# Both halves of layer 1 as Strassen products from the seventh chunk on, sums grown on copies in PSUM, and layer 2 in two PSUM banks

## The chip, the cores and the metric

The kernel runs on one core of one Trainium2 chip. The metric is device time in microseconds (us) for one execution. Before the change three runs gave 208.86, 209.4 and 210.07 us; the median is 209.4 us.

## What is computed

Inputs are q, k, v of shape (4, 8, 768, 64) (batch, heads, positions, head size), a norm gain of 512, and two weight matrices of 512 x 2048 and 2048 x 512; the output is float32 of shape (4, 768, 512).

```
scores = (q @ k.T) / sqrt(64), kept where the key is one of the first 4
         positions, or lies 0 to 127 positions behind the query
x   = softmax(scores) @ v, heads side by side           (4, 768, 512)
xn  = (x - mean(x)) / sqrt(var(x) + 1e-6) * g_ln
out = x + relu(xn @ w_ch1) @ w_ch2
```

Nearly all of the arithmetic is in the last line: layer 1 (512 to 2048, with relu) and layer 2 (2048 to 512).

## The kernel before

The 3072 rows are cut into 24 tiles of 128 rows and 12 chunks of two tiles, three chunks to a batch. In the code chunks count from 0: "the seventh chunk" is c = 6. The kernel has no loop on the chip. It creates some 1100 operations (`P.op`, line 84), each with the engine or engines that can do it, the buffers that it reads, writes or holds, and a function that emits its instructions. `Plan.run` (line 115) gives each an engine, a start and a place in the rings of buffers, by priorities and assumed costs; the program is emitted in the order of those starts (lines 1210 to 1238), and each engine executes its own part strictly in that order. The framework adds the semaphores for what an instruction reads and overwrites.

The engines are TensorE (PE, matmuls), VectorE (DVE), ScalarE (ACT), GpSimd (POOL) and SyncE (SP, which issues DMAs). PSUM has eight banks of 512 float32 columns: four in the two tiles of the ring `pair` (attention), four in the ring `one` (all else).

Per chunk, from c = 4 on:

- **Attention** (`attend`, line 777): scores by PE in two groups `sc..0`, `sc..1` (line 802), exp on ACT (814), mask on DVE or POOL (826, 821), sink values `sv` (721), values `av` (854), then on DVE the division (`rc`, `x`: 868, 870), mean and variance (`bn`, `ag`: 874, 876), and the normed rows `xc` (885); a transposing DMA makes `xnt`, 512 x 256 in bf16.
- **Layer 1** (`mlp`, line 1006, and `halves`, line 927). The 2048 columns lie in two halves g = 0, 1, of 1024 columns each, that end in the tiles `hq[0]` and `hq[1]`. The first half is a Strassen-type scheme of seven products m1 to m7 (line 958) instead of eight: 2 x 2 blocks of weights (512 columns by 256 inputs) against 2 x 2 blocks of tokens (128 by 256 inputs), with sums of weight blocks (`wsum`, line 923, once) and of token blocks (`xt`, on POOL, line 938, once per chunk). A product is eight matmuls of 128 columns. It uses three banks z, w, y: m1, m6, m7, m4 grow in z, m5 and m3 in y, m2 is alone in w. Between them ACT copies a bank to `tz` (969) for later use, DVE adds a bank and a `tz` into `hq` (980), and ACT clips that block at zero in place (983); the last block is clipped straight out of the bank (1001). The second half is plain: four units `ph` of eight 256-column matmuls (1027), each followed by one relu out of the bank, `rl` (1037 on ACT, 1039 on DVE).
- **Layer 2** (`wino`, line 1074, from c = 2 on): seven products p1 to p7 of eight 256-column matmuls (line 1109), with sums of blocks of `hq` (s1 to s4 for both halves, DVE, line 1092) and of the second weights (made once). It has four regions of 256 columns: z in the bank x, l2 and r1 in the bank y, l1 in the bank w. p1, p6, p5 grow in z, p7 and p4 in l2; p2 is l1 and p3 is r1. A `keep` (DVE, line 1123) adds a region and the rows x into a buffer `tm` in SBUF, a `final` (DVE, line 1130) adds a region and a `tm` into the output tile `ot`. Four of each make the chunk's two output tiles, which SP stores.

The order of PE's work before, from one chunk's end to the next, is regular: p1 p2 p7 p6 sc p4 p5 p3 of a chunk, then m1 sv av m5 m2 ph av m6 m3 ph m7 ph ph m4 of the next chunk, then that chunk's p1. After the last chunk's p3 there is one small matmul `late` (line 1206) that reads the last output, and the program ends with a branch on a flag.

Of the kernel before, what the change touches and what calls it, by code (L numbers as in the profile page):

```python
# [13 lines left out]
class Buf:  # L14


    def __init__(self, name, ring=None):
        self.name, self.ring = name, ring
        self.writers, self.users = [], []
        self.slot = None  # L20
        self.left = 0
# [6 lines left out]
class Unit:  # L28


    def __init__(self):
        self.free_at = 0.0
        self.lives = []
        self.held = False


class Slot:
# [12 lines left out]
    def take(self):  # L50
        for u in self.units:
            u.held = True
# [12 lines left out]
class Plan:  # L65


    SEM = 0.035
    TO_PE = 0.11
    PE_DRAIN = 0.18  # L70
    SWITCH = 0.095
    LANES = 8
    SHARED = 36.0
    MIXED = 1e9
    DMA_BUSY = {}
# [32 lines left out]
    def lat(self, src, dst):  # L108
        if src.eng == "PE" and src.dma is None:
            return -self.PE_DRAIN if dst == "PE" else self.SEM  # L110
        return self.TO_PE if dst == "PE" else self.SEM

    WINDOW = {"PE": 0.2, "ACT": 0.25, "DVE": 0.25, "POOL": 0.25, "SP": 0.0}

    def run(self):
        free = {"PE": 0.9, "ACT": 0.75, "DVE": 0.9, "POOL": 1.5, "SP": 0.75}
        lanes = {"POOL": [0.0] * self.LANES, "HW": [0.0] * self.LANES}
        n_dma = {"POOL": 0, "HW": 0}
        dma_free = {"POOL": 0.0, "HW": 0.0, "all": 0.0}
        mode = "n"  # L120
        ready = [o for o in self.ops if o.n_wait == 0]
        order = []
        tensor = sorted((o for o in self.ops if "PE" in o.engs), key=lambda o: (o.prio, o.seq))
        while ready:
            while tensor and tensor[0].start is not None:
                tensor.pop(0)
            head = tensor[0] if tensor else None
            cand = {}
            first = min([o.prio for o in ready for b in o.bufs if b.ring == "pair" and b.slot is None], default=1e9)
            for o in ready:  # L130
                if "PE" in o.engs and o is not head and o.prio >= PAR["strict"]:
                    continue
                need = [b for b in o.bufs if b.ring and b.slot is None]
                ok, avail, took = True, 0.0, {}
                for b in need:
                    used = [u for s in took.values() for u in s.units]
                    ss = [s for s in self.rings[b.ring] if not s.held and not any(u in used for u in s.units)
                          and not (s.lent and o.prio > first)]
                    if not ss:
                        ok = False  # L140
                        break
                    since = max([min(s.free_at for s in ss)] + [min(free[e] for e in o.engs) - 0.3])
                    s = min((s for s in ss if s.free_at <= since), key=lambda s: (s.rank, s.free_at))
                    took[b] = s
                    avail = max(avail, s.free_at)
                if not ok:
                    continue
                best = None
                for e, (occ, lat) in o.engs.items():
                    r = max([free[e], o.nb, avail + (self.TO_PE if e == "PE" else self.SEM)]  # L150
                            + [d.end + self.lat(d, e) for d in o.deps])
                    if e == "PE" and o.mode_in != mode:
                        r = max(r, free[e] + self.SWITCH)
                    if o.dma is not None:
                        q = "POOL" if e == "POOL" else "HW"
                        r = max(r, lanes[q][n_dma[q] % self.LANES])
                    if best is None or r + lat < best[0] - 1e-9:
                        best = (r + lat, e, r)
                cand.setdefault(best[1], []).append((best[2], o, took))
            if not cand:  # L160
                stuck = sorted(ready, key=lambda o: o.prio)[:8]
                raise RuntimeError("plan stuck: " + ", ".join(
                    f"{o.name}[{','.join(b.name for b in o.bufs if b.ring and b.slot is None)}]" for o in stuck))
            e = min(cand, key=lambda e: min(c[0] for c in cand[e]))
            t0 = min(c[0] for c in cand[e])
            st, o, took = min((c for c in cand[e] if c[0] <= t0 + self.WINDOW[e]), key=lambda c: (c[1].prio, c[1].seq))
            for b, s in took.items():
                b.slot = s
                s.take()
            o.eng, o.start = e, st  # L170
            occ, lat = o.engs[e]
            free[e] = st + occ
            if e == "PE":
                mode = o.mode_out
            if o.dma is None:
                o.end = st + lat
# [1103 lines left out]
```

## Time and profile before

| | us |
|---|---|
| median of three runs | 209.4 |
| lowest, highest | 208.86, 210.07 |
| span of the profiled execution, first to last instruction | 206.6 |
| the median above that span | 2.8 |

The profiled execution has no time of its own on the page beside its span; the 2.8 us are what the median of the runs shown has more. The granted TensorE clock of the core was 1.000 as a mean.

How to read the rows. The page begins with the busy time of each engine (PE for matmuls, PEld for weight loads, which run beside matmuls). In the rows by group, the order is line, engine, operation, `out<-in` by the program's names without numbers, shape and count; then busy us and mean ns of one; then the engine's idle time just before, and what ended it. In a timeline the first column is the start in us from the start of the span, the second the time to the group's end, and square brackets hold the idle time before and who ended it; matmuls overlap, so their price is the distance from one start to the next. In a windows row the window is followed by its length, then PE, PEld, DVE, ACT and POOL busy (with counts), the granted clock, the DMA share and GB/s. A row of waits says who waited for whom, us in total, how often, and the longest.

### The profile page before, as it was taken

The page shows a single profiled execution, that of the slowest core. Times are in us where ns is not written, and L with a number is a line of the kernel's source. Part 1 is how long each engine was busy: PE and PEld are TensorE (multiplying, and loading weights), DVE is VectorE, ACT ScalarE, POOL GpSimd, SP SyncE. Part 2 cuts the span into 40 slices and gives each one's busy share as a digit, 9 for nine tenths or more (in the row PEclk, how much of TensorE's full clock was granted, in tenths as well). Part 3 has the DMA queues.
Part 4 walks back from the last instruction along what each step waited for, and adds up shares of the span by engine and source line. Part 5 has one row for each costly group of instructions (what it writes and reads, how often), then busy time and mean ns, then how long its engine had stood idle before and what let it go on. Part 6 is the DMA issues. An engine that isn't in the chain of part 4 may idle for free.

```text
span 206.6 us, 6790 instructions
## 1 busy us (share of the span) xinstructions
PE 199.4 (97%) x2766; PEld 165.6 (80%) x2766; DVE 179.6 (87%) x437; ACT 119.7 (58%) x187; POOL 118.7 (57%) x170
## 2 busy tenths in 40 slices
PE   6888999999999999999999999999999999999994
PEld 2557996674698897898998988988988988988993
DVE  7589769899599899899989989989989989998693
ACT  3649477839555655666486486485486585560620
POOL 7977475279039029959649949968627229125000
PEclk9999999999999999999999999999999999999999
DMA  5999999999999999999999999899976411210302
GB/s 117 146 195 195 197 181 205 199 158 171 186 200 124 124 191 101 121 174 101 175 152 137 113 159 143 109 171 114 194 117 101 128 33 23 106 32 19 108 27 84
DMA packets 101341, 27.55 MB, mean 133 GB/s; under 512 B 89652, under 2 KB 99128, under 8 KB 101304
## 3 DMA queue, kind: packets, MB, share of 16 engines
q0 software_dynamic: 67712, 13.37, 81.7%
q1 hardware_dynamic: 33304, 13.43, 34.1%
q8 instruction: 22, 0.36, 0.7%
q10 hardware_dynamic: 288, 0.26, 0.4%
q14 instruction: 15, 0.12, 0.2%
HBM read 27.31 MB, written 6.29 MB: 163 GB/s over the span
## 4 chain that ended last, share of the span: by engine, by line
PE 90%; DMA 3%; DVE 3%; POOL 2%; issue 0%; DVEq 0%
PE one L1109 31%; PE one L1027 20%; PE one L958 12%; PE one L1058 7%; PE one L1020 7%; PE pair L854 5%; PE pair L802 4%; DMA n4b<-in_q_dram 3%; PE one L672 1%; PE pair L721 1%; POOL nat L626 1%; PE one L714 1%; DVE xnt L907 1%; DVE kq L595 1%; POOL vn L589 0%; DVE st L874 0%
## 5 line engine op out<-in xcount | busy, mean ns | idle before, releaser
L1027 PE MATMUL one<-xnt,w 128*128 128x256 bf16 x384 | 46.8, 273 | 0.0
L814 ACT ACTIVATE pe<-pair 128x1024 bf16<-128x1024 f32 (+1 forms) x40 | 36.3, 963 | 18.2 <-PE pair L802 18.2
L1037 ACT ACTIVATE hq<-one 128x512 bf16<-128x512 f32 x58 | 33.4, 590 | 17.9 <-PE one L1020 9.4
L1027 PEld LDWEIGHTS <-w 128*128 128x128 bf16 x384 | 36.3, 98 | 4.0
L1109 PEld LDWEIGHTS <-hs 128*128 128x128 bf16 x320 | 31.0, 98 | 4.0
L882 POOL TENSOR_SCALAR st<-st 128x1 f32<-128x1 f32 x24 | 6.4, 266 | 44.4 <-DVE rec L868 27.5
L826 DVE TENSOR_TENSOR pe<-pe,mask 128x1024 bf16<-128x1024 bf16 (+1 forms) x35 | 27.1, 799 | 1.6 <-ACT pe L814 1.4
L969 ACT COPY tz<-one 128x512 f32<-128x512 f32 x24 | 13.9, 585 | 20.6 <-PE one L958 19.2
L1109 PEld LDWEIGHTS <-hq 128*128 128x128 bf16 x240 | 22.2, 98 | 4.1 <-issue 0.5
L589 POOL DMA_DIRECT2D vn<-in_v_dram x24 | 21.9, 922 | 2.2 <-DMA w<-in_moe_w_ch_dram 1.2
L983 ACT ACTIVATE hq<-hq 128x512 bf16<-128x512 bf16 x24 | 15.1, 630 | 13.1 <-DVE hq L980 12.6
L1109 PE MATMUL one<-w,hq 128*128 128x256 bf16 x160 | 19.2, 273 | 0.0
L980 DVE TENSOR_TENSOR hq<-one,tz 128x512 bf16<-128x512 f32 x24 | 16.4, 684 | 1.9 <-PE one L958 1.0
L1130 DVE TENSOR_TENSOR ot<-one,tm 128x256 f32<-128x256 f32 x40 | 15.9, 412 | 2.1 <-PE one L1109 1.8
L1123 DVE TENSOR_TENSOR tm<-one,x 128x256 f32<-128x256 f32 x40 | 16.6, 414 | 1.2 <-PE one L1109 1.1
L870 DVE TENSOR_TENSOR x<-pair,rec 128x512 bf16<-128x512 f32 x24 | 16.6, 691 | 0.8
L874 DVE BATCH_NORM_STATS2 st<-x 128x6 f32<-128x512 bf16 x24 | 16.5, 687 | 0.2
L1020 PE MATMUL one<-xnt,w 128*128 128x128 bf16 x256 | 16.0, 219 | 0.5 <-DVE xnt L907 0.5
L687 POOL DMA_DIRECT2D nat<-in_q_dram x16 | 14.2, 893 | 3.7 <-DMA w<-in_moe_w_ch_dram 3.7
L938 POOL TENSOR_TENSOR xt<-xnt 128x256 bf16<-128x256 bf16 x16 | 12.2, 778 | 7.1 <-DMA xnt<-xc 7.0
L687 POOL DMA_DIRECT2D nat<-in_k_dram x16 | 14.8, 928 | 2.4 <-DMA w<-in_moe_w_ch_dram 2.4
L1020 PEld LDWEIGHTS <-w 128*128 128x128 bf16 x256 | 14.6, 98 | 1.6 <-issue 0.8
(130 smaller groups left out, 387.7 us busy)
## 6 DMA issues: line engine op xcount, KB each, us to landing
out_dram<-ot SPq DMA_DIRECT2D x17, 256.0 KB
w<-in_moe_w_ch_dram POOLq DMA_DIRECT2D x8, 512.0 KB, 12.8
vn<-in_v_dram POOLq DMA_DIRECT2D x24, 128.0 KB, 6.9
nat<-in_k_dram POOLq DMA_DIRECT2D x17, 128.0 KB, 4.6
nat<-in_q_dram POOLq DMA_DIRECT2D x17, 128.0 KB, 4.9
out_dram<-ot SPq DMA_DIRECT2D x14, 128.0 KB
kq<-nat SPq DMA_TRANSPOSE x32
xnt<-xc SPq DMA_TRANSPOSE x20
```

What stands on the lines that cost most here:

```text
L589: loads[b * RB + r, "v"] = P.op(f"vld{t}", {"POOL": (0.87, 0.9)}, prio, lambda e: G.dma_start(bv.t[:, :, 0:64], v[b, :, 128 * r:128 * (r + ...
L687: lambda e, nat=nat, ap=ap: G.dma_start(nat.t, ap), writes=[nat], dma=SW if c < 6 else (*SW[:2], PAR["llag"]), after=behind(c, 0 if soon e ...
L814: P.op(f"ex{c}{hp}", {"ACT": act(2 * n)}, d + 0.1 + 0.05 * j, lambda e, pp=pp, pb=pb: nc.scalar.activation(pb.t[:, :, 0:n], pp.t[:, :, 0:n ...
L826: V.tensor_mul(pb.t[:, :, 0:n], pb.t[:, :, 0:n], mm),
L870: P.op(f"x{t}", {"DVE": dve(512)}, d + xo + 0.11, lambda e: V.tensor_tensor(x.t.rearrange("p (a h c) -> p a h c", a=2, c=64), pv()[:, :, : ...
L874: P.op(f"bn{t}", {"DVE": fix(0.60)}, d + xo + 0.12, lambda e: V.bn_stats(st.t[:, 8:14], x.t), reads=[x], writes=[st, mv])
L958: nc.tensor.matmul(b.t[:, 128 * h:128 * h + 128], lhsT=lt[:, kk, 128 * h:128 * h + 128], rhs=rh[:, kk, :], start=first and h == 0 and kk = ...
L1020: nc.tensor.matmul(ph.t[:, 128 * s:128 * s + 128], lhsT=w1[u // 2][:, j, 128 * s:128 * s + 128], rhs=xnt.t[:, j, 128 * (u % 2):128 * (u % ...
L1027: nc.tensor.matmul(ph.t[:, 256 * s:256 * s + 256], lhsT=w1[ht // 4][:, j, 128 * (ht % 4):128 * (ht % 4 + 1)], rhs=xnt.t[:, j, :], start=j ...
L1037: nc.scalar.activation(hg.t[:, u % 4, :], ph.t, AF.Relu)
L1109: nc.tensor.matmul(at(r), lhsT=get(left, g)[:, v, s, :], rhs=rhs, start=first and n == 0, stop=n == 7, skip_group_check=True)
L1123: return P.op(f"tm{name}_{c}", {"DVE": dve(256, 1.14)}, pr - PAR["kp"], lambda e: V.tensor_tensor(tm[name].t, at(r), xs[i].t[:, sl], op=AL ...
```

## The change

- `Plan.run` no longer plans. Two tables stand in the kernel: `SCHEDULE`, an engine letter (P, A, V, G, S) and a start (in hundredths of an assumed us) for each of the now 1159 operations in the order of their creation, and `SLOTS`, the place of each buffer in its ring. The starts serve only as order. Up to the middle of layer 2 of c = 3 the order on PE is that of before; from there it is another, in the chunks whose operations are unchanged too.
- The ring `one` has four more places: the four halves of the `pair` tiles. `tz` has three buffers instead of two.
- For c = 6 to 11 `both` replaces `halves` and the four `ph` units: the Strassen scheme for each half g, with three banks each. The second half's weight sums are made once (`weight_sums(1)`, four DVE operations). A sum of a bank and a `tz` is one DVE operation that also clips at zero (`TENSOR_ADD_SAT`), with no relu behind it.
- For c = 7 to 11 ("seeds"): ACT copies m1's result from bank z into bank w, and m2 grows on that copy; the block is then clipped straight out of w (on ACT, but for one on DVE).
- Layer 2 for c = 6 to 11 has two banks: z and l2 in x, l1 and r1 in y. For c = 7 to 11, where before a `keep` put z + x into SBUF for l1 and for r1, DVE writes z + x into the region l1 or r1 itself (`seed`, the operations `sy`), p2 or p3 grow on it, and a plain copy `out_of` takes the region to `ot` (eight of the ten on ACT, two on DVE). t7 and t6 stay as they were.
- In numbers over the whole kernel: sums of a bank and a `tz` on DVE 24 before, 32 after, of which 26 are the clipping kind; relus `rl` of the last chunk on DVE three fewer; copies to `tz` or into a bank on ACT 24 before, 42 after; relus out of or within `hq` on ACT accordingly fewer.

The core of the diff:

```diff
-    P.ring("one", [Slot(ones[i], f"one{i}", [banks[4 + i]]) for i in range(4)])
+    P.ring("one", [Slot(ones[i], f"one{i}", [banks[4 + i]]) for i in range(4)]
+           + [Slot(pairs[i][:, j, :], f"half{i}{j}", [banks[2 * i + j]], 1, True) for i in range(2) for j in range(2)])
...
+        def total(n, bank, done, tz, pr):
+            outs[n] = Buf(f"{n}_{c}{g}")
+            o = P.op(f"c{n}_{c}{g}", {"DVE": dve(512, 1.14)}, pr, lambda e: V._custom_dve(
+                dve_ops.TENSOR_ADD_SAT, out=block(n), in0=banks_[bank].t.rearrange("p (i t) -> p i t", i=4),
+                in1=tz.t.rearrange("p (i t) -> p i t", i=4), s0=FMAX, s1=0.0),
...
+        m1 = product(1, "z", "a11", "b11", True, second[:1])
+        if seeds:
+            seed = Buf(f"sd{c}{g}")
+            o1 = P.op(f"sd_{c}{g}", {"ACT": act(512)}, T + pos[0] - PAR["tzp"], lambda e: nc.scalar.copy(banks_["w"].t, banks_["z"].t),
+                      reads=[m1], hold=[banks_["z"]], writes=[banks_["w"], seed])
+        else:
+            t1, o1 = snap(1, "z", m1)
+        m5 = product(5, "y", 0, "t0", True)
+        t5, o5 = snap(5, "y", m5)
+        m2 = product(2, "w", "a12", "b21", not seeds, [o1] if seeds else [])
...
+        m6 = product(6, "z", 1, "t1", False, [o1])
+        t2, o2 = snap(6, "z", m6)
+        m3 = product(3, "y", 3, "b22", False, [o5])
+        total("c12", "y", m3, t2, T + pos[5] - late_)
+        m7 = product(7, "z", 2, "t2", False, [o2])
+        o3 = total("c22", "z", m7, t5, T + pos[6] - late_)
+        m4 = product(4, "z", "a22", "t3", False, [o3])
+        clip("c21", "z", m4, T + pos[3] - PAR["tzp"], ("ACT",))
...
-        quick = halves(c, T, hq[0]) if strassen else None
-        for u in range(4 if strassen else 0, NH1 // 2):
+        tokens = token_sums(c, T) if strassen else None
+        quick = ([both(c, T, g, hq[g], tokens) for g in range(2)] if c >= PAR["new"] else [halves(c, T, hq[0], tokens)] if strassen else [])
+        for u in range(4 * len(quick), NH1 // 2):
...
-        bank = {n: Buf(f"bk{n}{c}", "one") for n in "xyw"}
-        reg = {"z": ("x", 0), "l2": ("y", 0), "l1": ("w", 0), "r1": ("y", 256)}
+        new = c > PAR["new"]
+        if c >= PAR["new"]:
+            bank = {n: Buf(f"bk{n}{c}", "one", full=True, seeded=new and n == "y") for n in "xy"}
+            reg = {"z": ("x", 0), "l2": ("x", 256), "l1": ("y", 0), "r1": ("y", 256)}
...
+        def seed(r, done, half, pr):
...
+            return P.op(f"sy{c}_{half}", {"DVE": dve(256, 1.14)}, pr - PAR["kp"], lambda e: V.tensor_tensor(
+                at(r), at("z"), xs[i].t[:, sl], op=ALU.add), reads=[done, xs[i]], hold=[bank["x"]] + ([] if fresh else [bank["y"]]),
+                writes=[b] + ([bank["y"]] if fresh else []))
...
+        if new:
+            d1 = product(0, "p1", "z", "a11", 0, lo, True)
+            k1 = seed("l1", d1, 0, u(0) - 2)
+            d2 = product(1, "p2", "l1", "a12", 1, lo, False, [k1])
+            out_of("l1", d2, 0, u(1) - 0.5)
+            d7 = product(2, "p7", "l2", "s3", 0, 2, False, [prods["p1"]])
+            k7 = keep("t7", "l2", d7, 3, u(2) - 2)
+            d6 = product(3, "p6", "z", "s2", 0, 1, False, [k1])
+            k6 = keep("t6", "z", d6, 2, u(3) - 2)
+            d4 = product(4, "p4", "l2", "a22", 0, 3, False, [k7])
+            final("l2", d4, "t6", 2, u(4) - 1)
+            d5 = product(5, "p5", "z", "s1", 0, 0, False, [k6])
+            final("z", d5, "t7", 3, u(5) - 1)
+            k5 = seed("r1", d5, 1, u(5) - 1.1)
+            d3 = product(6, "p3", "r1", "s4", 1, hi, False, [k5])
+            out_of("r1", d3, 1, u(6) - 0.9)
```

The order in which the table issues layer 2's products and the DVE operations on their banks (in brackets; ACT's and other work left out unless PE does it between products; t is a `keep`, "seed" an `sy`):

- c = 6: p1, sc, p2, [t1], p7, p6, [t7], sv, p4, [t6], p5, then others, [t5], m1 of c = 7, p3.
- c = 7: p1, p7, [seed l1], m1, p2, three of other work, p6, other work, [t6], three m, p5, [t7, seed r1], six m, p3, two m, p4.
- c = 8: p1, p7, [seed l1], m1, sc, [t7], p6, m2, [t6], two m, p4, m3, p5, much of c = 9's work with [seed r1] in it, p2, m4, p3.
- c = 9: p1, p7, [seed l1], p6, [t7, t6] beside sv and two av, p5, m1, p4, m5, [seed r1], m5, p2, nine m, p3.
- c = 10: p1, m4, [seed l1], m1, p2, eight of other work, p6, m4, [t6], two m, p5, two m, p7, [seed r1], m4, [t7], p1 of c = 11, p3, p4.
- c = 11: p1, p3 and p4 of c = 10, with [t7 of c = 10, the clip rc11, s1, s1, s2, seed l1, s2] on DVE in that time, p6, p7, [t6], p5, [t7], p4, [seed r1], p3, p2, [copy of r1], `late`, and on ACT the copy of l1.

More of the change, by code (lines that the diff above doesn't have):

```diff
@@ L33, in __init__ @@
         self.lives = []
-        self.held = False
+        self.held = self.full = False
 class Slot:
@@ L65 @@
 class Plan:
[L68 to L75, printed above, removed]
     def __init__(self):
@@ new lines, in run @@
+    def run(self):
+        engines = dict(P="PE", A="ACT", V="DVE", G="POOL", S="SP")
+        table = SCHEDULE.split()
+        assert len(table) == len(self.ops)
+        for o, entry in zip(self.ops, table):
+            o.eng, o.start = engines[entry[0]], int(entry[1:]) / 100
+            o.end = o.start + o.engs[o.eng][1]
+        for b, n in zip(dict.fromkeys(b for o in self.ops for b in o.bufs if b.ring), "".join(SLOTS.split())):
+            b.slot = self.rings[b.ring][int(n, 36)]
+            for u in b.slot.units:
+                u.lives.append((min(o.start for o in b.users), max(o.end for o in b.users)))
+        return sorted(self.ops, key=lambda o: (o.start, o.seq))
@@ L1051, in mlp @@
             for f in range(parts):
-                pc = Buf(f"pc{t}{f}", "one")
+                pc = Buf(f"pc{t}{f}", "one", full=parts == 1)
                 sl = slice(wd * f, wd * (f + 1))
@@ L1182 @@
     for c in range(NC):
-        if c == PAR["half"]:
-            weight_sums()
+        for g, n in enumerate(("half", "new")):
+            if c == PAR[n]:
+                weight_sums(g)
         mlp(c)
```

335 lines of the change are left out of this document (191 added, 144 removed).

## The prediction, made before the change was run

> **What bounds the kernel now.** I read the page's busy shares and chain first, then TensorE's waits, then the busy time by stage.
>
> ```profile
> span 206.6 us, 6790 instructions
> PE 199.4 (97%) x2766; PEld 165.6 (80%) x2766; DVE 179.6 (87%) x437; ACT 119.7 (58%) x187; POOL 118.7 (57%) x170
> PE 90%; DMA 3%; DVE 3%; POOL 2%; issue 0%; DVEq 0%
> ```
> ```profile
> PE pair L1236 <- DVE vn L487: 1.8, 1, 1.8
> ...
> PE one L1206 <- DVE ot L1130: 0.5, 1, 0.5
> ```
> ```profile
> 92.60:183.46 90.86, 90.86 (x1317) 80.39 (x1315) 84.40 (x201) 57.95 (x96) 57.66 (x83) 1.00 1.02 119
> ```
>
> TensorE (PE) carries 90% of the chain that ended last. Between 92.60 and 183.46, six chunks long, it is busy for 90.86 of 90.86 us at the full granted clock (1.00). Its waits are six, 1.8 us the longest; the one that ends the list is the closing `late` matmul. So PE is the bound without any slack: work taken from it is time won, and a wait put before it is time lost. VectorE (DVE) is busy for 84.40 of those 90.86 us; it is the next bound.
>
> The span is 206.6 us and the median of the three runs 209.4, so 2.8 us lie around the span. I sum against the span and add 2.8. Half a per cent, about 1 us, is what a measurement here tells from no change.
>
> **What is removed from PE.** For c = 6 to 11 the second half of layer 1 loses four units of eight 256-column matmuls and gains seven products of eight 128-column ones.
>
> ```profile
> 103.37 0.61 PE L958 MATMUL one<-xt,hq 128*128 128x128 bf16 x8
> 103.82 0.61 PE L958 MATMUL one<-xnt,hq 128*128 128x128 bf16 x8
> 104.27 1.04 PE L1027 MATMUL one<-xnt,w 128*128 128x256 bf16 x8
> 105.14 0.61 PE L958 MATMUL one<-xt,hq 128*128 128x128 bf16 x8
> 105.59 1.91 PE L1027 MATMUL one<-xnt,w 128*128 128x256 bf16 x16
> 107.33 0.61 PE L958 MATMUL one<-xt,w 128*128 128x128 bf16 x8
> ```
>
> The second column overlaps with the next row, so the price is the distance between starts: 0.45 us for a Strassen product, 0.87 for a direct unit (104.27 to 105.14; 1.74 for two). Per chunk 4 x 0.87 = 3.48 goes and 7 x 0.445 = 3.12 comes (0.44 to 0.45 between rows); times six that is **2.2 us less PE work**. Layer 2 keeps its seven products of eight matmuls, and attention its matmuls.
>
> **What moves between DVE and ScalarE (ACT).**
>
> ```profile
> L980 DVE TENSOR_TENSOR hq<-one,tz 128x512 bf16<-128x512 f32 x24 | 16.4, 684 | 1.9 <-PE one L958 1.0 <-ACT tz L969 0.4
> L1130 DVE TENSOR_TENSOR ot<-one,tm 128x256 f32<-128x256 f32 x40 | 15.9, 412 | 2.1 <-PE one L1109 1.8
> L1066 DVE SCALAR_TENSOR_TENSOR ot<-one,st,x 128x512 f32<-128x512 f32 x4 | 2.9, 736 | 0.0
> L923 DVE TENSOR_TENSOR hq<-w 128x1024 bf16<-128x1024 bf16 x1 | 0.7, 685 | 0.0
> L1039 DVE TENSOR_SCALAR hq<-one 128x512 bf16<-128x512 f32 x6 | 4.1, 689 | 0.2
> ```
>
> Sums with `tz` go from 24 to 32: +8 x 0.684 = 5.5 us. Four more weight sums: +2.7. One clip on DVE: +0.7. Of the ten output sums that become plain copies, eight go to ACT: -8 x 0.412 = -3.3. Three relus of the last chunk leave DVE: -2.1. Together DVE gets +3.5 us, against 206.6 - 179.6 = 27 us idle, and ACT, busy 58%, is changed by little. I cost both at nothing on the path; the cover is DVE's idle time, and the second rival is what it costs when that is gone. Sums with the built-in clip, 26 of them, are an operation that before does not show. Bounds: 684 ns (the same shape, one operation) and 736 ns (L1066, two operations on a PSUM operand); below 684 nothing points, since the bytes are the same. I take 684; the upper end is 26 x 0.052 = 1.4 us of DVE. Seeds, which DVE writes to PSUM, before does not show either: I take the same sum into SBUF (`tm`, 0.41 us in the rows further down), with 0.34 (the distance of two starts there) and 0.69 (L1039) as ends; in the four turns below that hold a seed that is -0.3 to +1.1 us.
>
> **What is added: waits for a shared bank.** In the new layer 2, z and l2 lie in one bank and l1 and r1 in the other. What two engines do with one bank, even with different columns of it, shows at the start of the kernel, where L595 copies two column sets of one bank, one on ACT, one on DVE:
>
> ```profile
> 6.01 0.61 PE L649 MATMUL one<-ident,hq 128*128 128x128 bf16 x8
> 6.43 0.65 ACT L595 COPY kq<-one 128x256 bf16<-128x256 bf16 x2 [0.78 <-PE one L649]
> 6.84 0.76 DVE L595 COPY kq<-one 128x256 bf16<-128x256 bf16 x2 [1.04 <-ACT kq L595]
> ```
> ```profile
> L595 ACT COPY kq<-one 128x256 bf16<-128x256 bf16 x2 | 0.6, 375 | 0.8 <-PE one L649 0.8
> ```
> ```profile
> 194.77 0.63 ACT L983 ACTIVATE hq<-hq 128x512 bf16<-128x512 bf16 x1 [0.76 <-DVE hq L980]
> 195.30 0.68 DVE L980 TENSOR_TENSOR hq<-one,tz 128x512 bf16<-128x512 f32 x1
> ```
>
> Both copies needed the same transposes. ACT began at 6.43 and needed 0.37; DVE stood idle for 1.04 us and began at 6.84, and its wait is put down to ACT. The targets are different parts of a tile in SBUF, which alone holds nobody back: at 195.30 DVE writes one block of `hq` while ACT, until 195.40, still writes another. So it is the bank: accesses of two engines go one after the other, in the order in which the program issues them. The Trainium skill says likewise (PSUM — Partial Sum Buffer, section PSUM bank collisions raise a hardware error): two engines must not touch one bank and quadrant at once, another address in the bank is no help, and compilers order such pairs. That is its rule against this change, and the rows above agree with it.
>
> Before, each reader had its bank: p7 wrote l2's while DVE read z's. Now the new order issues, for instance, p7 and behind it the sum that reads p6's z; that sum must wait for all of p7, and the p5 behind it for the sum. The price of such a turn:
>
> ```profile
> 199.02 0.41 DVE L1123 TENSOR_TENSOR tm<-one,x 128x256 f32<-128x256 f32 x1
> 199.35 0.41 DVE L1092 TENSOR_TENSOR hs<-hs,hq 128x512 bf16<-128x512 bf16 x1
> 199.68 0.41 DVE L1130 TENSOR_TENSOR ot<-one,tm 128x256 f32<-128x256 f32 x1
> ...
> 201.50 1.04 PE L1109 MATMUL one<-n4b,hs 128*128 128x256 bf16 x8
> ...
> 202.37 1.04 PE L1109 MATMUL one<-w,hs 128*128 128x256 bf16 x8
> ...
> 202.57 0.42 DVE L1123 TENSOR_TENSOR tm<-one,x 128x256 f32<-128x256 f32 x1 [0.45 <-PE one L1109]
> 202.91 0.96 DVE L1130 TENSOR_TENSOR ot<-one,tm 128x256 f32<-128x256 f32 x2
> ...
> 203.93 0.19 PE L1206 MATMUL one<-ones_f,ot 128*1 128x1 f32 x2 [0.52 <-DVE ot L1130]
> ```
>
> A product takes 0.87. DVE starts 0.20 behind its last start-slot (202.37 to 202.57), works 0.41, and PE follows 0.06 later (202.91 + 0.96 = 203.87 to 203.93). **A turn is 0.67 us**, less what PE has to do in between; a DVE operation queued in between adds 0.34 (199.02 to 199.35).
>
> ```profile
> 112.16 0.25 PE L802 MATMUL pair<-kq,kq 64*64 64x64 bf16 x4
> ...
> 112.63 1.05 PE L1109 MATMUL one<-w2t,hq 128*128 128x256 bf16 x8
> ...
> 115.80 0.29 PE L721 MATMUL pair<-vs,ps 32*128 32x260 bf16 x4
> 116.02 0.66 PE L854 MATMUL pair<-vn,pe 128*128 128x65 bf16 x16
> ```
>
> So scores fill 0.47 and sink values 0.22. Through the new order, DVE's operations in brackets:
> - c = 6: p1, scores, p2, [five others, t1], p7. DVE: 0.20 + 0.61 + 4 x 0.34 + 0.41 + 0.06 = 2.64; PE has 0.47 + 0.87 = 1.34 behind p1, so up to 1.3, but those five were partly issued ahead of p1; I take 0.4. Then p6, [t7], sink values, p4: 0.67 - 0.22 = 0.45. Then p4, [t6], p5: 0.67. Sum 1.5.
> - c = 7: p1, p7, [seed], m1, p2: 0.67 - 0.45 = 0.22.
> - c = 8: p7, [seed, s2, t7], m1, scores, p6: 0.67 + 2 x 0.34 - 0.45 - 0.47 = 0.43.
> - c = 9: p7, [seed], p6, nothing between: 0.67.
> - c = 10: work of chunk 11 lies in every turn: 0.
> - c = 11: p6, p7, [t6], p5, [t7], p4, [seed], p3, p2, and no other work is left to PE: three turns, 2.0. Ahead of it p6 needs the last s2, the seventh of DVE's operations from the start of p1 on: 0.09 + 0.34 + 0.61 + 4 x 0.34 + 0.42 + 0.06 = 2.88, against PE's p1, p3, p4 of 3 x 0.87 = 2.61: 0.2 to 0.3, taken as 0.2 (0.09 is what DVE is late with the seed of r1 behind p7: 0.20 + 0.34 - 0.45).
>
> That is 5.0 us of new waits on PE. At the end, both outputs of the second bank are read after p2, first on DVE, then on ACT: 0.20 + 0.41 + 0.06 + 0.37 = 1.04, where before the last product's end (203.24) stood 0.63 ahead of the last output (203.87): +0.4.
>
> Behind a waiting DVE sum stand the next chunk's attention and layer-1 sums, in order, and behind a waiting product all of PE; so PE's waits are not made up for.
>
> **Sum:** -2.2 + 5.0 + 0.4 = +3.2: span 209.8, time **212.6 us**. Bounds of the waits: every turn at nothing (the first rival), and c = 6's first at 1.3.
>
> **Rivals.**
> - *No order within a bank between a write and a read of other columns* (the other side). The L595 rows show two reads and no PE write, so the rule need not hold PE. Then t6 runs beneath p7, and so on; of the waits 0.2 is left, the end is 0.20 + 0.37 = 0.57 behind p2, and the sum is -2.2 + 0.2 - 0.06 = -2.1: 207.3. It decides as soon as all new waits on PE stay under 1.8 us. Against it: DVE's 1.04 us at 6.84. Chance 0.22.
> - *DVE becomes the bound as well.* In the six-chunk stretch it has 6.46 us idle. About 3.4 of the 3.5 us of added work falls there, PE's part shrinks by 2.2, the clipped sums may cost 1.4 more, and waits at banks hold DVE itself for some 3 to 4 us (c = 8 and 9: a whole product each). That makes 84.4 + 3.4 + 1.4 + 3.5 = 92.7, 1.8 over today's 90.86, and with the last chunk's 2.0 + 0.2 + 0.4 the sum is +4.4: 213.8. Against it: back to back, DVE's operations start 0.34 apart and last 0.41, so its busy share overstates its load. Chance 0.12.
> - *Only the last chunk waits*, the middle being covered: -2.2 + 2.2 + 0.4 = +0.4: 209.8. For it: c = 10, where the order covers every turn. Chance 0.16.
> - The forecast: 0.50.
>
> Faster by over 0.5%: 0.22 (the first rival). Within: 0.16 (the third). Slower: 0.62. Leaving out the first rival alone would leave out more than 2 in 10, so the range reaches from just below it to 1.2 us above the DVE rival, about what dearer seeds add: 207.0 to 215.0. The forecast's own range, with c = 6's first turn at 0 or 1.3 and the seeds' ends, is 211.9 to 214.6.
>
> **What would show it.** PE's busy time down by about 2.2 us. In the list of PE's waits, rows that name DVE sums of layer 2 (`tm`, seeds), some 5 us in all, none of which before has. In the last chunk's timeline three gaps of 0.6 to 0.7 between products, each ended by a DVE sum that itself started 0.2 behind a product of other columns. If such a sum starts beneath a running product of its bank, my main step is wrong and the time is near 207.3. If gaps name `hs` or `hq` sums instead, DVE's load is the cause. A clipped sum well over 736 ns would refute its bound.

## The result and the profile after

The changed kernel takes 227.8 us (median of 4 runs, 226.6 to 228.1), the kernel before 209.7 us beside it: a ratio of 1.087, 95% interval 1.082 to 1.092. The forecast was 212.6 us, with a range up to 215.0: the sign was right, the size was not. The profiled execution has a span of 226.1 us, 19.5 us more than before, and its TensorE clock is 0.998.

Here is the page of the changed kernel: the span, the busy times, and the shares of the chain that ended last.

```profile
span 226.1 us, 7085 instructions
...
PE 203.7 (90%) x2910; PEld 166.3 (74%) x2916; DVE 188.8 (83%) x439; ACT 119.2 (53%) x189; POOL 117.7 (52%) x170
...
PE 65%; DVE 25%; issue 4%; ACT 3%; DVEq 0%; ACTq 0%
```

Before, TensorE (PE) carried 90% of that chain and VectorE (DVE) 3%. Now DVE carries a quarter of it. PE's busy time is 203.7 us for 199.4, where the forecast's first sign was a fall of some 2.2. That is no more work: the row of a product lasts 1.03 us although the next can start 0.87 behind it, and wherever a gap follows, this overhang counts as busy. So I go by the starts below. The same six-chunk window that was filled to 90.86 of 90.86 us has holes (columns: window, its length, then busy time and count of PE, PE's weight loads, DVE, ScalarE, GpSimd, then clock, DMA share, GB/s):

```profile
92.60:183.46 90.86, 83.11 (x1293) 71.89 (x1292) 85.04 (x186) 51.60 (x85) 55.16 (x76) 1.00 1.11 111
```

The list of PE's waits of the changed kernel says what ended them (what waited, for whom: total us, times, longest):

```profile
PE one L1186 <- DVE tm L1200: 2.8, 6, 0.9
PE pair L1343 <- DVE vn L473: 1.8, 1, 1.8
PE one L1186 <- DVE one L1215: 1.6, 3, 0.6
PE one L1186 <- DVE hs L1164: 1.5, 2, 1.2
PE pair L1186 <- DVE tm L1200: 1.0, 2, 0.5
PE pair L1017 <- ACT hq L1048: 1.0, 1, 1.0
PE pair L1017 <- DVE hq L1039: 1.0, 1, 1.0
PE pair L1100 <- DVE hq L972: 0.7, 1, 0.7
PE pair L1017 <- ACT tz L1028: 0.6, 2, 0.4
...
PE pair L1017 <- DVE x L856: 0.5, 1, 0.5
PE pair L1017 <- DVE one L1215: 0.5, 1, 0.5
```

L1186 is layer 2's products, L1200 the kept sums `tm`, L1215 the seeds, L1164 the sums `hs`. These rows the forecast asked for. It did not ask for the rows with L1017, the Strassen products of layer 1, which wait here for readers of data that is not theirs: for the attention output `x`, whose operand last stood in their bank, and for a seed of layer 2, which reads the bank beside theirs.

To see how much is waiting and how much is work, I took the start of every PE operation from the start of p1 in chunk 4 to the start of the closing `late` product, and counted as a gap each distance between the starts of two neighbouring matmuls of different operations that is over 0.2 us, less 0.11. What is left of the stretch is PE's work.

| kernel | stretch, us | gaps | rest |
|---|---|---|---|
| before | 110.2 | 2.0 | 108.2 |
| changed | 125.8 | 18.7 | 107.1 |

So the 19.5 us are: p1 of chunk 4 starts 1.1 later (94.82 for 93.75), PE's work is 1.1 less, the gaps are 16.7 more, and from the start of `late` to the end of the span it takes 5.5 for 2.7, 2.8 more.

With the place of each product in the banks (from `SLOTS`) the 18.7 us of gaps divide so: 6.0 are the turns that the forecast named; 7.1 end with an access to the other bank of the tile that the product writes, or to both (a tile of the ring `pair` has two banks; `e6_eight_tiles` below); some 2 are of the kind that before had too. Most of the 3.6 left end with VectorE, the largest being p6 of chunk 7 (1.34) and p2 of chunk 10 (0.68).

### The profile page after: what moved, and what is told of

It reads as the page before. It is cut to its first block, busy times and chain, and to the rows that moved or that the text cites. A ratio compares the mean times of both kernels' runs of the same rounds, so it can differ in the third digit from the quotient of the medians.

```text
span 226.1 us, 7085 instructions
## 1 busy us (share of the span) xinstructions
PE 203.7 (90%) x2910; PEld 166.3 (74%) x2916; DVE 188.8 (83%) x439; ACT 119.2 (53%) x189; POOL 117.7 (52%) x170
## 4 chain that ended last, share of the span: by engine, by line
PE 65%; DVE 25%; issue 4%; ACT 3%; DVEq 0%; ACTq 0%
PE one L1186 16%; PE one L1100 7%; PE one L1131 6%; PE one L1017 6%; DVE hs L1164 6%; PE pair L1017 5%; PE one L1092 5%; PE pair L1186 4%; PE pair L840 4%; PE pair L788 2%; DVE tm L1200 2%; DVE pe L812 2%; DVE hq L1039 2%; DVE x L856 2%; ACT tz L1028 2%
## 5 line engine op out<-in xcount | busy, mean ns | idle before, releaser
L1186 PEld LDWEIGHTS <-hs 128*128 128x128 bf16 x320 | 30.1, 98 | 12.2 <-issue 6.4
L1110 ACT ACTIVATE hq<-one 128x512 bf16<-128x512 f32 x32 | 19.1, 598 | 20.2 <-PE one L1100 10.5
L868 POOL TENSOR_SCALAR st<-st 128x1 f32<-128x1 f32 x24 | 5.9, 248 | 42.0 <-DVE st L862 26.0
L1186 PEld LDWEIGHTS <-hq 128*128 128x128 bf16 x240 | 22.4, 98 | 5.7 <-issue 2.6
L1017 PEld LDWEIGHTS <-hq 128*128 128x128 bf16 x384 | 22.9, 98 | 3.3 <-issue 1.8
L812 DVE TENSOR_TENSOR pe<-pe,mask 128x1024 bf16<-128x1024 bf16 (+1 forms) x35 | 24.2, 711 | 1.0 <-ACT pe L800 0.9
L1017 PEld LDWEIGHTS <-w 128*128 128x128 bf16 x288 | 17.6, 98 | 3.8 <-issue 2.6
L1186 PE MATMUL one<-w,hq 128*128 128x256 bf16 x144 | 18.4, 273 | 0.6 <-DVE one L1215 0.6
L1164 DVE TENSOR_TENSOR hs<-hq 128x512 bf16<-128x512 bf16 x40 | 17.6, 464 | 1.1 <-ACT hq L1048 0.6
L1100 PE MATMUL one<-xnt,w 128*128 128x256 bf16 x152 | 18.1, 273 | 0.0
L869 POOL TENSOR_TENSOR st<-st,mhalf 128x1 f32<-128x1 f32 x24 | 14.6, 609 | 2.0
L1131 PE MATMUL one<-w,hq 128*128 128x512 bf16 x60 | 14.8, 380 | 0.2
## 6 DMA issues: line engine op xcount, KB each, us to landing
w<-in_moe_w_ch_dram POOLq DMA_DIRECT2D x8, 512.0 KB, 13.1
```

The lines of the kernel that those rows point to most:

```text
L812: V.tensor_mul(pb.t[:, :, 0:n], pb.t[:, :, 0:n], mm),
L1017: nc.tensor.matmul(b.t[:, 128 * h:128 * h + 128], lhsT=lt[:, kk, 128 * h:128 * h + 128], rhs=rh[:, kk, :], start=first and h == 0 and kk = ...
L1100: nc.tensor.matmul(ph.t[:, 256 * s:256 * s + 256], lhsT=w1[ht // 4][:, j, 128 * (ht % 4):128 * (ht % 4 + 1)], rhs=xnt.t[:, j, :], start=s ...
L1110: nc.scalar.activation(hg.t[:, u % 4, :], ph.t, AF.Relu)
L1131: nc.tensor.matmul(pc.t[:, 0:wd], lhsT=(hq[s // 2].t[:, (2 * s + i) % 4, 128 * ii:128 * ii + 128] if by_tile else hq[ht // 8].t[:, ht // 2 ...
L1164: P.op(f"{n}_{c}{g}", {"DVE": dve(512, 0.52)}, T - PAR["sp"][g] + PAR["sq"][i], lambda e, n=n, x0=x0, x1=x1, g=g, op=op: V.tensor_tensor(s ...
```

## Experiments

Each ratio is to the kernel before, run beside that experiment. There are three theories. **Theory 1**: the turns through the shared banks of layer 2, as the forecast priced them, with what they delay. **Theory 2**: VectorE, with more work and a queue worked down in order. **Theory 3**, formed after the first four runs: the two banks of one pair tile are kept in order like one bank. Beside these, a theory of the end. Where a run gives l2 a bank of its own, the seeded banks of a later Strassen product hold other values (one product in chunk 7, in `e1_own_bank` one more in chunk 10); the amount of work is the same.

### e4_two_banks_only: the turn by itself

The kernel before with only layer 2's banks of the change:

```
-        reg = {"z": ("x", 0), "l2": ("y", 0), "l1": ("w", 0), "r1": ("y", 256)}
+        two = c >= 6
...
+        reg = ({"z": ("x", 0), "l2": ("x", 256), "l1": ("y", 0), "r1": ("y", 256)} if two else
+               {"z": ("x", 0), "l2": ("y", 0), "l1": ("w", 0), "r1": ("y", 256)})
...
```

Left out here: the buffer of the third bank goes, and p7 and p3 no longer start their bank anew.

> The kernel before, in its own order, with one part of the change alone: layer 2 of chunks 6 to 11 in two banks (z beside l2, l1 beside r1), without Strassen products in the second half, without seeds. In its order p7 and p6, and p4 and p5, stand back to back, and p6 and p4 nearly. Theory 1: a turn from TensorE to VectorE and back costs 0.67 us less the TensorE work between the two products: 1.46, 1.48, 1.45, 1.46, 1.77 and 2.01 us in the six chunks, 9.6 us in all: 219.3 us, 218 to 221 us. Theory 2 (shared banks cost little; VectorE's load is the cause of the loss): under 212 us.

Measured: 218.0 us against 208.9, a ratio of 1.042 (1.035 to 1.048): 9.1 us for an expected 9.6, and the gaps, counted as above, are 9.1 us more than before. In its last chunk (timeline, PE and DVE; start, length, what; in brackets the idle time ahead and what ended it):

```profile
208.31 1.03 PE L1111 MATMUL one<-n4c,hs 128*128 128x256 bf16 x8 [0.52 <-DVE tm L1125]
209.86 1.03 PE L1111 MATMUL one<-w2t,hq 128*128 128x256 bf16 x8 [0.52 <-DVE tm L1125]
```
```profile
209.38 0.42 DVE L1125 TENSOR_TENSOR tm<-one,x 128x256 f32<-128x256 f32 x1 [0.46 <-PE one L1111]
```

Products of 0.87 stand 1.55 apart, and the sum between them starts 0.20 behind the last start-slot of a product that writes other columns. The turn and its price hold.

### e1_own_bank: the turns taken out of the changed kernel

```
-        new = c > PAR["new"]
+        new, own = c > PAR["new"], {6: 2, 9: 3, 10: 4, 11: 4}.get(c)
...
+            if own is not None:
+                bank["v"] = Buf(f"bkv{c}", "one", full=True, fixed=own)
+                reg["l2"] = ("v", 0)
...
```

> The changed kernel, in its own order, but l2 of layer 2 gets a bank to itself in chunks 6, 9, 10 and 11 (one that stands free there), so that p7 and p4 no longer share a bank with z. Theory 1 (turns through a shared bank made the time): the gaps ahead of p7, p6, p4 and p5 in these chunks, 2.2 us in chunk 6, 1.1 us in chunk 9 and 2.05 us in chunk 11, go, and what was late behind them comes earlier: 220.0 to 222.5 us against 227.8 us. Theory 2 (VectorE, fuller than before and working down its queue in order, is the bound between 100 us and the tail): only the tail's 2.05 us go, and the rest comes back as waits for sums: 225.0 to 226.0 us.

Measured: 224.9 us, ratio 1.073 (1.066 to 1.081), so about 2.8 us less than the changed kernel's 1.087: between the two expectations. Chunk 6's turns went for the most part; p4 still waits for `tmt7` (0.60). But the last chunk's three stood as before:

```profile
212.62 1.03 PE L1191 MATMUL pair<-n4b,hs 128*128 128x256 bf16 x8 [0.52 <-DVE tm L1205]
214.17 1.03 PE L1191 MATMUL pair<-w2t,hq 128*128 128x256 bf16 x8 [0.52 <-DVE tm L1205]
```
```profile
213.69 0.42 DVE L1205 TENSOR_TENSOR tm<-pair,x 128x256 f32<-128x256 f32 x1 [0.79 <-PE pair L1191]
```

There z lies in `half01` and l2 in `half00`: two banks, but one tile, `pair0`. DVE's sum of one bank waits for the product in the other, and the next product for the sum. That made theory 3. With it I went through the gaps of the changed kernel: those ended by an access to the other bank of the same pair tile sum to 7.1 us. In 0.7 of them, m5 of chunk 7, the reader is `x`, which reads both banks, the product's own too.

### e5_short_statistics: less work on VectorE

```
-        P.op(f"bn{t}", {"DVE": fix(0.60)}, d + xo + 0.12, lambda e: V.bn_stats(st.t[:, 8:14], x.t),
+        P.op(f"bn{t}", {"DVE": fix(0.60)}, d + xo + 0.12, lambda e: V.bn_stats(st.t[:, 8:14], x.t[:, 0:64] if c >= 6 else x.t),
```

> The changed kernel with bn_stats of the tokens of chunks 6 to 11 taken over 64 of the 512 columns (the mean and variance are so left out in the main): 12 instructions of 0.684 us on VectorE fall to about 0.2 us, 5.8 us less VectorE work, none of it in a sum that TensorE waits for directly. Theory 2 (VectorE's queue is the bound): the sums behind come earlier, and the time falls by 3 to 6 us, to 222 to 225 us. Theory 1: TensorE's waits are the turns and stay: within 1 us, 226.8 to 227.8 us.

Measured: 226.4 us, ratio 1.083 (1.075 to 1.090), by the ratios some 0.8 us less than the changed kernel; that is inside the uncertainty. Theory 2 did not get its 3 to 6 us, as long as the turns were there.

### e6_split_control and e6_eight_tiles: one tile for each bank

An instruction that reads both banks of a pair needs one tile, so those are cut in two in both runs; only the second has eight tiles. `Two` is a small class that hands out two tiles under one name. The eight tiles stand in the order of the old ones, one to a bank.

```
-    pairs = [psum.tile([128, 2, 512], FP32, name=f"pair{i}") for i in range(2)]
+    low = [psum.tile([128, 512], FP32, name=f"low{i}") for i in range(4)]
+    pairs = [Two(low[2 * i:2 * i + 2]) for i in range(2)]
...
-                pb.t, pp.t, AF.Exp, scale=scale), reads=[pp], writes=[pb])
+                pb.t[:, h2, :], pp.t[:, h2, :], AF.Exp, scale=scale) for h2 in range(2)], reads=[pp], writes=[pb])
...
```

> The changed kernel, but every instruction that reads both banks of a pair tile (the exponentials, the reciprocals and the scaled copies x) is cut into one for each bank; the pair tiles stay tiles of two banks. It is the control of the next run. VectorE gets 24 more reciprocals of some 0.14 us and 24 more copies (two of 0.41 us in place of one of 0.68 us), some 7 us spread over the span, ScalarE 40 more exponentials. All theories: 0 to 3 us above the changed kernel, 227.8 to 231 us.

> The same cut instructions, and PSUM is eight tiles of one bank each in place of two pair tiles of two banks and four of one: the borrowed half banks of the Strassen products have no neighbour in their tile any more. Theory 3 (two banks of one tile are kept in order against each other like one bank: a product in one waits for VectorE's or ScalarE's read of the other, and the read for the product): the gaps of the changed kernel that end with an access to the neighbouring bank, 7.1 us between chunk 5 and chunk 11, go: 7 to 9 us below the control, 219 to 223 us. Theories 1 and 2 (bank turns, VectorE's load) as the whole: within 1 us of the control.

Measured: control 227.6 us, ratio 1.088 (1.080 to 1.096); eight tiles 222.6 us, 1.065 (1.057 to 1.074). The tiles alone are worth 5.1 us; 7 to 9 were expected. The gaps fell from 18.7 to 13.1. Theory 3 holds; its price was 2 us too high, since where a false wait went, a true one often stood close behind: the gap of m7 in chunk 10 fell from 1.06 to 0.42, where it waits for a copy out of its own bank. The control cost nothing here: VectorE's busy time on its page is 189.5 for 188.8 us, not some 7 more.

One false wait, first in the changed kernel, then in `e6_eight_tiles`. m4 of chunk 8's second half is written to `half00`; ScalarE clips m4 of the first half out of `half01`:

```profile
159.13 0.60 ACT L1048 ACTIVATE hq<-pair 128x512 bf16<-128x512 f32 x1
...
159.78 0.61 PE L1017 MATMUL pair<-xt,w 128*128 128x128 bf16 x8 [0.96 <-ACT hq L1048]
```
```profile
158.29 0.61 PE L1027 MATMUL low<-xt,w 128*128 128x128 bf16 x8
...
158.64 0.60 ACT L1058 ACTIVATE hq<-low 128x512 bf16<-128x512 f32 x1
```

With one tile for both banks the product waits for the clip's end at 159.73; with two tiles it starts before the clip, which then runs beneath it.

### e7_eight_own_bank: both, and e12_own_bank_again

The edits of the last two sections together (own bank in chunks 6, 10 and 11; in 11 now a single tile), with `o11_0` on VectorE.

> Eight tiles of one bank, and l2 of layer 2 in a bank of its own in chunks 6, 10 and 11, and the last output copy on VectorE. In the tail of e1_own_bank l2 and z had different banks of one pair tile, and the three turns of 0.68 us stood as before; here they have tiles of their own. Theory 3 with theory 1: the tail's three turns go (2.0 us) and chunk 6's 2.2 us: 4 us below e6_eight_tiles, 215 to 219 us. If turns are a matter of anything else than the tile: above 221 us.

> e7_eight_own_bank once more, on the same chip as e11_one_last_store, so that the two can be set against each other: 217.3 to 218.3 us.

Measured: 217.8 us, ratio 1.043 (1.035 to 1.051), 4.8 us below eight tiles alone (3.4 of it are gaps, and in these two profiles the end is 1.3 shorter, see below); in a second set of runs 218.4 us, 1.045 (1.041 to 1.050). The last chunk's turns are gone (PE, then DVE):

```profile
206.87 1.04 PE L1201 MATMUL one<-n4a,hs 128*128 128x256 bf16 x8
207.74 1.04 PE L1201 MATMUL low<-n4b,hs 128*128 128x256 bf16 x8
208.61 1.04 PE L1201 MATMUL one<-w2t,hq 128*128 128x256 bf16 x8
```
```profile
207.14 0.40 DVE L1215 TENSOR_TENSOR tm<-low,x 128x256 f32<-128x256 f32 x1
208.01 0.42 DVE L1215 TENSOR_TENSOR tm<-one,x 128x256 f32<-128x256 f32 x1
```

Products follow each other at 0.87, and the sum at 207.14 runs beneath the product that started at 206.87. In the eight tiles z and l2 touch nothing in common. Gaps: 9.7.

### e9_light_vector: VectorE again, with most turns gone

`e7_eight_own_bank` with the statistics cut as in `e5_short_statistics`, and with narrow sums of `hq`:

```
+        w = 32 if c >= 6 else 128
-                    sb[n, g].t, get(x0, g), get(x1, g), op=op),
+                    sb[n, g].t[:, :, :, 0:w], get(x0, g)[:, :, :, 0:w], get(x1, g)[:, :, :, 0:w], op=op),
```

> e7_eight_own_bank with less work on VectorE from chunk 6 on: bn_stats over 64 of 512 columns (12 instructions, 0.5 us less each) and the eight sums of layer 2's operands in each chunk over 32 of every 128 columns (48 instructions, 0.42 to 0.59 us down to about 0.2 us); the rest of the statistics and of the sums is left out. Some 18 us less VectorE work of 138 us in that stretch. Theory 2 (with the shared banks and tiles gone, the waits that are left are VectorE's queue, which runs back to back from 131 to 150 us): most of the 7 us of gaps that are left from chunk 6 on go: 211 to 214 us against 217.8 us. Rival (the order puts products nearer to what they need than the chain from TensorE over ScalarE to TensorE takes, whatever VectorE's load): 215.5 to 217.5 us.

Measured: 214.0 us, ratio 1.027 (1.020 to 1.034), 3.4 to 3.9 us below `e7_eight_own_bank` (by the ratios and by the medians); gaps 4.8. So with most turns gone VectorE does hold up TensorE. One of its waits, the longest left in `e7_eight_own_bank`, shows how. This is the same place in the changed kernel, chunk 7's p6 and the last `hs` sums that it needs:

```profile
147.35 0.72 POOL L925 TENSOR_TENSOR xt<-xnt 128x256 bf16<-128x256 bf16 x1
...
148.14 0.87 POOL L925 TENSOR_TENSOR xt<-xnt,xt 128x256 bf16<-128x256 bf16 x1
148.42 0.88 DVE L1164 TENSOR_TENSOR hs<-hq 128x512 bf16<-128x512 bf16 x1
...
148.98 0.84 POOL L925 TENSOR_TENSOR xt<-xnt 128x256 bf16<-128x256 bf16 x1
...
149.22 1.69 DVE L1164 TENSOR_TENSOR hs<-hs,hq 128x512 bf16<-128x512 bf16 x2
...
149.79 0.84 POOL L925 TENSOR_TENSOR xt<-xnt,xt 128x256 bf16<-128x256 bf16 x1
...
150.97 0.28 PE L1186 MATMUL one<-n4c,hs 128*128 128x256 bf16 x1 [1.23 <-DVE hs L1164]
```

Three sums that take 0.42 us each in the tail take 0.85 to 0.88 here, beside GpSimd's token sums, and p6 waits 1.23 us for them. Narrow sums nearly close this gap (counted as above, 1.34 in both kernels with full sums, 0.21 here). The run can't part the two things it changes, VectorE's load and the length of the sums that TensorE waits for directly; that stays open.

### e10_before_split: VectorE's room in the kernel before

The same cuts as in the control, put into the kernel before.

> The kernel before, in its own order and its own banks, with the reciprocals, the scaled copies x and the exponentials cut in two like in e6_split_control: some 7 us more work on VectorE and some 4 us on ScalarE, spread over the span, and nothing else. If VectorE had room for the 3.5 us that the change adds to it (the forecast cost them at nothing): within 1 us of 208.8 us. If a fuller VectorE by itself makes TensorE wait (theory 2): 212 us or more.

Measured: 210.5 us against 208.5, ratio 1.009 (1.005 to 1.013). On the pages VectorE's busy time rose by 2.1 us (181.7 for 179.6) and ScalarE's by 2.8, and the time by 2.0. Its gaps are 4.1 us for 2.0. It lies between the two expectations: VectorE and ScalarE did not have room for the additions at no cost, but it is not 212 either. Which of the two engines made the gaps, or the longer way from scores to attention values, this run can't part.

### The end: e2_last_on_vector, e8_code_moved, e11_one_last_store

```
-P20167 A20276   (p2 of chunk 11; its copy o11_0, on ScalarE)
+P20167 V20276   (e2: the copy on VectorE)
+P19860 A19967   (e11, on top of e7: p2 behind p7, the copy on ScalarE in the middle of the tail)
-S20318
+S20040          (e11: the store of that half ahead of the others)
```
```
+    for _ in range(106):     (e8: in the branch that is never taken)
+        T.matmul(ones[0][:, 0:128], lhsT=ident, rhs=ident, start=True, stop=True)
```

> The changed kernel with one instruction moved: the last copy of an output half out of PSUM, o11_0, is done by VectorE instead of ScalarE. Theory of the end (ScalarE, which has now work up to the last microsecond, reaches its branch late and the span waits 2.5 us at the end of the program for it): ScalarE is through with its branch before the last store, and the time falls by 2.2 to 2.6 us, to about 225.4 us. Rival (the end waits for the stores, not for the branch): no change within 0.3 us.

> The changed kernel, with 106 products (212 instructions) added to TensorE's part of the branch that is never taken; nothing that runs is changed, only the place of the code behind the branch. In the changed kernel TensorE's branch at the end takes 3.78 us, before it took 0.39 us, and the span ends 5.1 us after the last output copy in place of 2.7 us. Theory of the code's place (the target, which lay at instruction 6438 before and lies at 6738 now, is no longer in what was fetched ahead): the branch takes about 0.4 us again, and 2.4 us less in all, 225.4 us. Rival (anything else of the longer program): 3.8 us and 227.8 us again.

> e7_eight_own_bank with the product p2 of the last chunk moved from the last place on TensorE to the place behind p7, its output copy o11_0 back on ScalarE in the middle of the tail, and its store ahead of the others: as in the kernel before, one output half and one store are left behind the last product, not two. Theory (of the end's loss of some 2.4 us, one copy of 0.34 us and one store issue of 0.4 us with its transfer come from the second half that is ready only at the end): 0.8 to 1.3 us less than e7_eight_own_bank, 216.5 to 217.0 us. Rival (the end waits only for the branch or for a fixed time behind the last product): within 0.4 us of it.

Measured: e2 226.5 us, ratio 1.082 (1.074 to 1.090), not the 225.4 expected; e8 227.2 us, 1.087 (1.079 to 1.094), no change. Neither theory of the end held as it was put: TensorE's branch took 3.78 and 3.74 us in these two as well. e11 took 217.0 us, ratio 1.038 (1.034 to 1.042), against 218.4 us of the same program without this edit beside it (`e12_own_bank_again`): 1.4 us, a little more than the 0.8 to 1.3 expected; in the two profiles a stalled branch, in the table below, adds to the difference. The time from the start of `late` to the end of the span, with the length of TensorE's branch, sorts the profiles:

| kernel | `late` to the end, us | branch on TensorE, us |
|---|---|---|
| before, e4, e10 | 2.7, 2.8, 2.7 | 0.39 each |
| e11 (one half last) | 2.9 | 0.50 |
| e7 (two halves last) | 4.2 | 0.51 |
| e12, the same program as e7 | 5.7 | 3.98 |
| changed, e2, eight tiles, e9 | 5.5 each | 3.8 each |

Two output halves behind the last product in place of one are 1.3 us (4.2 for 2.9), a branch that stalls is 1.3 to 1.5 more. SyncE's queue shows it as a wait at the end, first in the changed kernel, then in `e12_own_bank_again`:

```profile
SPq L1382 <- PEq L1347: 2.5, 1, 2.5
```
```profile
SPq L1397 <- PEq L1362: 2.7, 1, 2.7
```

The profile of `e7_eight_own_bank` has no such row. So the stall is no matter of the code's place in the program alone; one program had it in one profile and, on another chip, not in the other. In `e6_split_control` TensorE's branch took 0.50 us and the end 5.5 all the same: there ScalarE, which still has `o11_0` as its last work, came out of its own branch 4.0 us after it began. The theory of ScalarE was thus right for that profile, but taking its copy away is no use where TensorE stalls. The Trainium skill (Runtime: NRT & Kernel Launch, section Instruction fetch mechanics) says that a taken branch whose target is not in the blocks already fetched waits for a DMA that fetches it; a stall that comes or does not, and is then nearly always of one length, agrees with that. What decides it was not found.

## Why the prediction was wrong

The forecast was -2.2 +5.0 +0.4 = +3.2 on the span; it became +19.5. The sign came out by the mechanism that the forecast named, since those turns alone outweigh the work that PE was spared; the size did not. Step by step:

- **PE's work, -2.2**: -1.1 (108.2 to 107.1 outside the gaps; 106.9 in `e9_light_vector`). The prices of 0.45 and 0.87 hold between rows; where the other half went, into seams under 0.2 us or elsewhere, was not tried.
- **The price of a turn, 0.67**: right. `e4_two_banks_only` cost 9.1 of 9.6 us, and the last chunk's three gaps are 0.68, 0.68 and 0.69. Its rows of the changed kernel, beside those the forecast showed of before:

```profile
215.03 1.03 PE L1186 MATMUL pair<-n4b,hs 128*128 128x256 bf16 x8 [0.52 <-DVE tm L1200]
216.58 1.03 PE L1186 MATMUL pair<-w2t,hq 128*128 128x256 bf16 x8 [0.52 <-DVE tm L1200]
218.14 1.03 PE L1186 MATMUL one<-w,hs 128*128 128x256 bf16 x8 [0.52 <-DVE one L1215]
```

- **Which turns, 5.0**: the named ones came as named and were 6.0 us: chunk 6 2.2 for 1.5, chunk 7 0.19 for 0.22, chunk 8 0.83 for 0.43, chunk 9 0.69 for 0.67, chunk 11 2.2 for 2.2. Only turns with several VectorE operations queued in them were priced too low.
- **"So it is the bank"**: the first step that failed. The rows of L595 show two engines at one bank, and that bank lay in one tile. From them I read a rule about banks; the order is kept for the whole tile, also between its two banks. The change puts Strassen sums into halves of the pair tiles, next to the attention's scores and outputs and next to each other, and I gave that no price. For chunk 10, where the forecast says "work of chunk 11 lies in every turn: 0", the gaps of both layers are 4.9 us, 4.1 of them ended by the neighbouring bank. Another 0.7 is a turn that was taken as covered: ahead of the seed that p2 waits for, VectorE had the three instructions of `guard` (195.57 to 197.47), which the list of the order leaves out. `e6_eight_tiles` against its control puts the whole at 5.1 us. The Trainium skill's rule that the forecast cites (PSUM — Partial Sum Buffer, section PSUM bank collisions raise a hardware error) is about one bank and quadrant; it gives no reason for this order. The order is the program's own: only the tiles differ between `e6_eight_tiles` and its control.
- **VectorE's and ScalarE's additions at nothing**: the second step that failed. The new operations themselves cost what was bounded:

```profile
L1039 DVE CUSTOM_DVE_ANT_0 hq<-one,tz 128x512 bf16<-128x512 f32 x14 | 9.3, 683 | 1.6 <-ACT tz L1028 1.2 <-PE one L1017 0.3
...
L1039 DVE CUSTOM_DVE_ANT_0 hq<-pair,tz 128x512 bf16<-128x512 f32 x12 | 8.1, 688 | 3.4 <-ACT tz L1028 2.5 <-PE pair L1017 0.7
...
L1215 DVE TENSOR_TENSOR one<-one,x 128x256 f32<-128x256 f32 x6 | 2.6, 427 | 1.1 <-PE one L1186 1.1
```

  684 was taken for the clipped sum, 0.41 for the seed. VectorE's busy time rose all the same by 9.2 us (179.6 to 188.8), not by 3.5. The sums `hs` of two blocks of `hq`, 40 in both kernels, take 464 ns in the mean for 418 before, the 24 rows `xc` 518 for 416, the four new weight sums 0.7 to 1.1 us each for 0.68; the forecast took every old price over as it was.

  And the 27 us of idle time that were to hide the additions are no cover: `e10_before_split` shows that 2.1 us more on VectorE and 2.8 on ScalarE already cost the old kernel 2.0, and `e9_light_vector` that lighter work on VectorE is worth 3.4 to 3.9 us once most turns are gone. What the change's own additions cost by themselves no run measures, nor what its order costs with the old banks; that stays open. The rival "DVE becomes the bound as well" named this, with chance 0.12 and at 213.8 us, as it counted the load and not what a sum's lateness does to products that stand right behind it.
- **The end, +0.4**: +2.8. The two last output halves are 1.3 us of it, where the forecast counted only the second copy and not the second store; the branch is the rest, and the forecast gave it no price.
- **The rivals**: "no order within a bank" is refuted by the rows at 215.03 to 218.14: each product waits for a sum out of other columns of its bank. "Only the last chunk waits" is refuted too, since chunk 6 alone lost 2.2 us.

Taken together from the top: the changed kernel 1.087 of before, one tile for each bank 1.065, l2 in its own bank 1.043, lighter sums on VectorE 1.027. The 5.1 us that its span still is over the old one are 2.9 in the end, 1.5 in the stretch (2.8 more gaps, 1.3 less work) and 0.7 ahead of it. No version with the change's order came near the kernel before.

## What to carry to other kernels

Before you let two users share storage, ask what unit their order is kept for: here it was the tile and not the bank, and half a tile lent to another stage tied that stage's products to readers it had nothing to do with. Price a wait for a sum by the whole queue ahead of the sum, and don't take idle time of an engine that is 87% busy as cover for anything that TensorE waits for soon. A product order is tuned to the waits that it was made for; when storage is shared anew, look for products that now stand back to back in one tile, each cost a turn of 0.67 us here.

## What the runs showed of the hardware

- VectorE's sums of two bf16 operands in SBUF slow down beside GpSimd's: of the `hs` sums of the changed kernel from 98 us on, the 29 that overlap a GpSimd instruction take 0.59 us in the mean (the 11 beside nothing but its DMA issues 0.46), the other 29 take 0.42. The Trainium skill (SBUF — State Buffer, section Who interferes with whom) says that a VectorE instruction with two SBUF inputs contends with a GpSimd instruction that reads SBUF; the rows at 148.42 to 150.91 agree.
- The branch at the end of TensorE's program takes 0.39 to 0.51 us or 3.7 to 4.0 us, even with the same program. ScalarE came out of its own 2.5 to 4.1 us after it began, in every profile; the program hints at the branch ahead of time for TensorE and VectorE alone. A copy that is ScalarE's last work is followed by this time.
- A 512-column VectorE sum out of PSUM with a clip built in takes no longer than the plain sum: 683 to 688 against 684 ns.
